# Delta-rule attention and an exact-GELU feed-forward on one core: nine runs of small matrix products fewer, K S tied tile by tile to the joins

## The chip, the cores and the metric

The kernel runs on one core of one Trainium2 chip. The metric is the device time of one execution in microseconds (us). Before the change three runs gave 630.46, 628.44 and 628.91 us, so the median is 628.91 us. Everything is computed in 32-bit floating point.

## The reference

Two layers follow each other. The first is a delta rule with a state of 48 x 48 for each of 4 x 8 heads, over 768 tokens; the second is a feed-forward layer with the exact GELU over the 3072 tokens.

```python
k_n = k / (np.linalg.norm(k, axis=-1, keepdims=True) + 1e-06)
for t in range(768):
    y[:, :, t] = q_t @ state
    state = state + beta_t * outer(kn_t, v_t - kn_t @ state)
x = y.transpose(0, 2, 1, 3).reshape(3072, 384)
h = x @ w_in                      # 384 x 2048
g = 0.5 * h * (1 + erf(h / sqrt(2)))
out = g @ w_out                   # 2048 x 384
```

## The kernel before

The 768 tokens are cut into 12 chunks of 64. For each chunk the recurrence becomes small products for each head. `grams` (L439, PSUM tile `psG`) multiplies the keys with themselves; its results go to SBUF by ACT (L601 for the later chunks). From the Gram blocks of a pair of chunks, GpSimd eliminates triangular blocks of 32; DVE then turns them (L538, L542). `join_both` puts blocks of 32 together to blocks of 64 in two levels. Both levels are products of 32 rows by 64 columns (L650, `psJ`). Level 0 is read from PSUM by eight DVE multiplications (L662, into `XM`), level 1 by eight DVE copies (L666, into `Zf`). Which of them are issued is said by `take`, one half of the heads at a time. Level 1 reads `XM`, so it follows all of L662.

With the inverse in hand a chunk `c` takes four steps. `against_state` multiplies the keys with the state and with the queries (L731, `psK`; one PSUM tile for each of the two halves of the batch); `subtract` turns it into `V` and `P` on DVE (L764, L767, L771: three instructions for each half). `solve` first multiplies the queries with the state (L751, `psQ`, copied to `y` by two ACT copies at L755), then applies the inverse (L791, `psU`, copied to `U` by ACT at L799 and L801). `outputs` computes P U and the state's update (L821 and L832, `psY`), and `turns` transposes the result (L883). These four together are `state_steps`, with further steps tied behind the solve if `second` names them.

All these products are small: they use a quarter or an eighth of TensorE's array at a time. The tiles `psG`, `psJ`, `psK`, `psQ`, `psU` and `psY` of the small products take turns in two PSUM buffers (`dn`), so that each new tile waits for the readers of the tile before the last one.

Between them stand the large products of the feed-forward layer, on the whole array. They are cut by a scheme with fewer multiplications. `part_of_layer` (L1023; tiles `psX`, `psZ`, `psY`, `psV`) does eleven products of the first layer for each block, named P1, P5, P6, P2, R22, R11, P7, P3, R12, P4, R21 in this order. After P6, DVE adds into `psY` (L1051) and then reads it again (`add_p5`, L1082); P7 accumulates into the same tile and so waits for both. After P7, DVE forms one half (L1059), and ACT applies the GELU to it; after R12 it forms another (L1071), again with a GELU behind it. `mix` (L1090, L1091 and further lines) adds and subtracts activations for the second layer (L957), whose weights and sums come ready.

The order is written out by hand: every step has a time in a list `plan` (chunk number plus a fraction), and `emit` calls the steps in the order of these times. The queues of DVE and GpSimd stand in exactly that order. TensorE's and ACT's order is the scheduler's, with two exceptions: `together` ties all TensorE instructions of its steps into one unbroken run, and `behind` keeps the large products in their own order. A loop over `w` = 4, 6, 8, 10 plans a pair of chunks each: the joins of the pair, chunk `w` and chunk `w + 1`, the Grams of chunks `w + 2` and `w + 3`. The names `begins` and `takes` hold the times of the joins, of the two chunks' steps and of the takes.

Of the kernel before, what the change touches and what calls it, by code (L numbers as in the profile page):

```python
# [19 lines left out]
def kernel(  # L20
# [35 lines left out]
    NA = B // 2  # L56
# [38 lines left out]
    tiles = {}  # L95
# [616 lines left out]

    SIDES = [(0, 0), (1, 0), (0, 1), (1, 1)]

    def against_state(us):

        for u in us:
            u.W = u.V
            u.y = None
            if u.c == 0:  # L720
                nc.gpsimd.tensor_tensor(u.W, u.V,
                                        ng[:, u.a].unsqueeze(2).to_broadcast([128, H, D]),
                                        op=ALU.mult)
                continue
            w = D if u.c == 1 else D + C
            psK = dn("psK")
            u.psK = psK[:, :, 0:NP * w].rearrange("q r (j d) -> q r j d", d=w)
            for j in range(NP):
                for r, p in QUADS:
                    rows = slice(r * C, r * C + D)  # L730
                    nc.tensor.matmul(u.psK[HALF[p], r, j, :], lhsT=u.Kt[rows, p, j, :],  # L731
                                     rhs=SQ[rows, u.a, p ^ r, j, 0:w], start=True, stop=True)
            if u.c == 1:
                u.psQ = psK[:, :, NP * D:2 * NP * D].rearrange("q r (j d) -> q r j d", d=D)
                against_queries([u])
        if us[0].c > 2:
            subtract(us)

    def against_queries(us):
# [430 lines left out]
    def at(first, last, steps):  # L1170

        total, done, timed = sum(s[0] for s in steps), 0.0, []
        for w, *step in steps:
            timed.append((first + (last - first) * (done + 0.5 * w) / total, step))
            done += w
        return timed
# [122 lines left out]
    def state_at(c, *times, first=(), second=(), last=()):  # L1299

        steps = state_steps(c, first, second, last)
        if len(times) > len(steps):
# [25 lines left out]
             at(2.7, 2.701, [(1.0, together, join1[1]), (0.0, copy_out, "join", 4)]),  # L1328
             at(2.75, 2.751, [(1.0, together, join1[2]), (0.0, copy_out, "join", 4)]),
             state_at(2, None, 2.772, 2.851, 2.906, 2.922),  # L1330
             at(2.728, 2.729, [(1.0, norms, 4), (1.0, prep, 4)]), at(3.045, 3.046, [(1.0, together, (grams, [tiles[4, a] for a in range(NA)]))])]
    plan += [at(1.07, 1.071, [(1.0, load_v, 2)]), at(2.727, 2.728, [(1.0, sum_of_w, 1, 2)]), at(2.96, 2.961, [(1.0, last_sum_of_w)]), at(3.07, 3.071, [(1.0, sum_of_w, 4)])]
    plan += [at(c + 0.958, c + 0.959, [(1.0, mix_x, c)]) for c in (2, 3, *range(4, NC, 2))]
    plan += [at(t, t + 0.1, v_steps(c)) for c in range(4, NC)
# [6 lines left out]
    for c in range(4, NC):  # L1341
        us = [tiles[c, a] for a in range(NA)]
        even = c % 2 == 0
        for name, src, t in (("Kb", k, {4: 1.8, 5: 2.73, 6: 3.25, 7: 3.55}.get(c, c - (2.9 if even else 3.6))),
                             ("Qb", q, {4: 3.2, 5: 3.9}.get(c, c - (1.4 if even else 1.29)))):
            plan += [at(t, t + 0.01, [(1.0, load_blocks, c, name, src)])]
        for name, t in (("Kn", {4: 2.1, 5: 2.74, 7: 4.24}.get(c, c - (2.1 if even else 2.84))),
                        ("Kp", {4: 3.6, 5: 4.3}.get(c, c - (0.6 if even else 0.85)))):
            plan += [at(t, t + 0.01, [(1.0, load_k, c, name)])]
        t = {4: 2.7262, 5: 2.9595, 6: 3.5, 7: 4.38}.get(c, c - (2.7 if even else 2.98))  # L1350
        plan += [at(t, t + 0.0005, [(1.0, turned_k, u) for u in us])]
        t = {4: 3.88, 5: 4.452}.get(c, c - (0.47 if even else 0.77))
        plan += [at(t, t + 0.01, [(1.0, turned_q, u) for u in us])]
    def gram(c):
        return [(grams, [tiles[c, a] for a in range(NA)])] if c < NC else []
# [4 lines left out]
    def rows_of(g, w, pieces):  # L1360
        rows = eliminate_steps(g)
        assert sum(n for n, _, _ in pieces) == len(rows)
        parts, done = [], 0
        for n, first, last in pieces:
            parts += [at(w + first, w + last, rows[done:done + n])]
            done += n
        return parts
# [6 lines left out]
    for c in (2, 3, *range(4, NC, 2)):  # L1374
# [8 lines left out]
        else:  # L1383
# [1 line left out]
            plan += [at(c + x, c + x + 0.001, [(1.0, mix, c + 1, 1, h)]) for h, x in enumerate((2.3, 2.36))]  # L1385

    plan += [at(3.19, 3.191, [(1.0, transposed, u, (1,)) for u in fourth]),
             at(3.1, 3.101, [(1.0, together, *gram(5))]),
             at(2.93, 2.931, [(1.0, norms, 5)]), at(2.961, 2.962, [(1.0, prep, 5)]),
             at(3.11, 3.111, [(1.0, finish, 4)]),  # L1390
             state_at(3, 3.367, 3.59, 3.72, 3.93)]
# [2 lines left out]
    for w in range(4, NC, 2):  # L1394
        more_to_come = w + 2 < NC
        if w == 4:
            begins = 0.21, 0.29, 0.36, 0.45, 0.53, 0.63, 0.67, 0.77, 0.86, 0.93
            takes = 0.212, 0.214, 0.292, 0.294
            n6, p6, n7, p7, f7 = 0.2, 0.26, 0.4, 0.44, 0.55
        else:  # L1400
            begins = -0.305, -0.163, -0.06, 0.08, 0.21, 0.29, 0.38, 0.52, 0.67, 0.84
            takes = -0.304, -0.303, -0.16, -0.158
            n6, p6, n7, p7, f7 = 0.15, 0.2, 0.27, 0.32, 0.44
            t = -1.555 if w > 6 else -1.44
            plan += rows_of(w // 2, w, ((1, t, t + 0.001), (1, t + 0.02, t + 0.021), (1, t + 0.03, t + 0.031),
                                        (31, t + 0.04, t + 0.84), (1, -0.42, -0.419), (1, -0.331, -0.3305),
                                        (1, -0.33, -0.3295)))
        begins = [w + t for t in begins]
        if w == 4:
            one = [tiles[w, a] for a in range(NA)]  # L1410
            plan += [[(t, (together, step)) for t, step in (
                (begins[0], (join_both, 2, 0)), (begins[1], (join_both, 2, 1)),
                (w + 0.335, *gram(w + 2)), (begins[2], (against_state, one[:1])),
                (w + 0.405, (against_state, one[1:])), (w + 0.49, *gram(w + 3)))],
                     state_at(w, None, *begins[3:6])]
        else:
            plan += [at(begins[0], begins[0] + 0.001, [(1.0, together, (join_both, w // 2, 0))]),
                     at(begins[1], begins[1] + 0.001, [(1.0, together, (join_both, w // 2, 1), *gram(w + 2))]),
                     state_at(w, *begins[2:6], second=gram(w + 3))]
        plan += [state_at(w + 1, *begins[6:], second=())]  # L1420
        plan += [at(w + t, w + t + 0.001, [(1.0, take, i % 2)]) for i, t in enumerate(takes)]
        if more_to_come:
            late_ = 0.02 if w == 4 else 0.0
            plan += spread("gram", 2, begins[1] + 0.04 + 1.5 * late_) + spread("gram", 2, begins[1] + 0.06 + 1.5 * late_)
            plan += spread("gram", 4, begins[3] + 0.04 + late_)
            plan += [at(w + n6, w + n6 + 0.001, [(1.0, norms, w + 2)]), at(w + p6, w + p6 + 0.001, [(1.0, prep, w + 2)]),
                     at(w + n7, w + n7 + 0.001, [(1.0, norms, w + 3)]), at(w + p7, w + p7 + 0.001, [(1.0, prep, w + 3)]),
                     at(w + f7, w + f7 + 0.001, [(1.0, finish, w + 2)])]
# [32 lines left out]
```

## Time and profile before

| what | value |
|---|---|
| median of three runs | 628.91 us (628.44 to 630.46) |
| the profiled execution's own time | 629.47 us |
| its span | 627.7 us |
| TensorE matmul (PE), busy | 606.6 us, 97%, 8358 records |
| VectorE (DVE), busy | 428.5 us, 68% |
| ScalarE (ACT), busy | 240.6 us, 38% |
| GpSimd (POOL), busy | 212.8 us, 34% |
| mean granted clock of TensorE | 0.986 of full speed |

The span is the stretch from the first to the last instruction that the profile shows; 1.77 us of the execution's time lie outside it. One 32-bit product is two records of a matmul, one transpose is one. [...] In the timeline a row holds consecutive instructions of one line and one tile; a mark in brackets gives the idle time before the row and what ended it.

### The profile page before, as it was taken

The page shows a single profiled execution, that of the slowest core. Times are in us where ns is not written, and L with a number is a line of the kernel's source. Part 1 is how long each engine was busy: PE and PEld are TensorE (multiplying, and loading weights), DVE is VectorE, ACT ScalarE, POOL GpSimd, SP SyncE. Part 2 cuts the span into 40 slices and gives each one's busy share as a digit, 9 for nine tenths or more (in the row PEclk, how much of TensorE's full clock was granted, in tenths as well). Part 3 has the DMA queues.
Part 4 walks back from the last instruction along what each step waited for, and adds up shares of the span by engine and source line. Part 5 has one row for each costly group of instructions (what it writes and reads, how often), then busy time and mean ns, then how long its engine had stood idle before and what let it go on. Part 6 is the DMA issues. An engine that isn't in the chain of part 4 may idle for free.

```text
span 627.7 us, 19675 instructions
## 1 busy us (share of the span) xinstructions
PE 606.6 (97%) x8358; PEld 541.4 (86%) x8358; DVE 428.5 (68%) x793; ACT 240.6 (38%) x546; POOL 212.8 (34%) x316
## 2 busy tenths in 40 slices
PE   6779999999999999999999999999999999999997
PEld 4667886776899999998899998899998899988997
DVE  6999899999867598564859555859546946422432
ACT  3476876615443255224451134452134222044200
POOL 4045002000379821885222884223884200000000
PEclk9985999999999999999999999999999999999999
DMA  9695766001423452453123533013321001000011
GB/s 135 155 284 145 162 146 180 23 3 38 74 38 47 78 92 35 69 105 39 16 45 54 101 62 38 12 33 62 64 50 18 11 2 28 8 19 1 0 26 26
DMA packets 159575, 39.63 MB, mean 63 GB/s; under 512 B 151168, under 2 KB 154368, under 8 KB 159488
## 3 DMA queue, kind: packets, MB, share of 16 engines
q1 hardware_dynamic: 156816, 37.34, 30.9%
q10 hardware_dynamic: 2672, 1.03, 0.8%
q8 instruction: 66, 1.08, 0.7%
q14 instruction: 21, 0.17, 0.1%
HBM read 33.62 MB, written 4.72 MB: 61 GB/s over the span
## 4 chain that ended last, share of the span: by engine, by line
PE 81%; DVE 10%; DMA 4%; SPq 2%; issue 1%; ACT 1%; DVEq 0%
PE psX L957 13%; PE psY L1023 11%; PE psY L957 9%; PE psX L1023 8%; PE psV L1023 6%; PE psZ L1023 5%; PE psZ L957 4%; PE psV L957 4%; PE psK L731 3%; PE psO L924 3%; PE psG L439 2%; DMA w_raw<-in_moe_w_out_dram 2%; PE psH L906 2%; PE psY L821 2%; PE psU L791 2%; PE psQ L751 2%
## 5 line engine op out<-in xcount | busy, mean ns | idle before, releaser
L376 POOL TENSOR_TENSOR n<-n,half 128x16 f32<-128x16 f32 x10 | 30.9, 3091 | 176.1 <-DVE n L374 118.4
L529 POOL TENSOR_TENSOR Nu<-Nu,tmp 128x30 f32<-128x30 f32 (+14 forms) x120 | 65.7, 548 | 9.4
L527 POOL TENSOR_TENSOR tmp<-Nu 128x30 f32<-128x30 f32 (+14 forms) x120 | 62.5, 521 | 9.4
L1023 PE MATMUL psX<-xT,w_in_sb 128*128 128x256 f32 (+1 forms) x288 | 62.5, 346 | 0.0
L957 PE MATMUL psX<-w_out_sb,G 128*128 128x192 f32 x320 | 56.4, 329 | 0.0
L957 PEld LDWEIGHTS psX<-w_out_sb,G 128*128 128x128 f32 x320 | 52.1, 190 | 0.8
L1023 PEld LDWEIGHTS psX<-xT,w_in_sb 128*128 128x128 f32 x288 | 47.9, 191 | 5.3
L906 PE MATMUL psH<-xT,w_in_sb 128*128 128x256 f32 x192 | 45.8, 395 | 0.7 <-ACT G L912 0.5
L906 PEld LDWEIGHTS psH<-xT,w_in_sb 128*128 128x128 f32 x192 | 37.1, 197 | 8.0 <-ACT G L912 1.4
L924 PE MATMUL psO<-w_out_sb,G 128*128 128x384 f32 x128 | 43.9, 490 | 0.0
L1051 DVE TENSOR_TENSOR psY<-psY,pu 128x512 f32<-128x512 f32 x20 | 14.0, 700 | 40.9 <-PE psY L1023 40.3
L1023 PE MATMUL psY<-xT,w_in_sb 128*128 128x256 f32 (+1 forms) x192 | 41.5, 345 | 0.0
L1006 ACT COPY pu<-psZ 128x512 f32<-128x512 f32 x40 | 23.5, 587 | 38.7 <-PE psZ L1023 36.3
L1006 ACT COPY xT<-psX 128x768 f32<-128x768 f32 x9 | 7.2, 799 | 81.1 <-PE psX L883 81.1
L924 PEld LDWEIGHTS psO<-w_out_sb,G 128*128 128x128 f32 x128 | 23.5, 190 | 14.2 <-issue 0.3
L1023 PEld LDWEIGHTS psY<-xT,w_in_sb 128*128 128x128 f32 x192 | 32.1, 191 | 3.5
L837 DVE TENSOR_TENSOR SQ<-SQ,psY 128x384 f32<-128x384 f32 x21 | 11.6, 552 | 32.5 <-PE psY L832 32.2
L1006 ACT ACTIVATE G<-G 128x512 f32<-128x512 f32 x40 | 25.2, 631 | 19.8 <-DVE G L1059 19.6
L1006 ACT ACTIVATE G<-psY 128x512 f32<-128x512 f32 x20 | 11.9, 596 | 47.4 <-PE psY L1023 47.4
L1059 DVE TENSOR_TENSOR G<-psY,pu 128x512 f32<-128x512 f32 x20 | 13.8, 690 | 22.2 <-PE psY L1023 21.5
L957 PE MATMUL psY<-w_out_sb,G 128*128 128x192 f32 x160 | 28.1, 329 | 0.0
L957 PE MATMUL psZ<-T,pu 128*128 128x192 f32 x160 | 28.1, 329 | 0.0
(204 smaller groups left out, 1374.6 us busy)
## 6 DMA issues: line engine op xcount, KB each, us to landing
Kp<-in_k_dram SPq DMA_DIRECT2D x76, 96.0 KB, 3.2
w_out_sb<-in_moe_w_in_dram SPq DMA_DIRECT2D x24, 256.0 KB, 5.5
w_raw<-in_moe_w_out_dram SPq DMA_DIRECT2D x16, 384.0 KB, 5.2
V<-in_v_dram SPq DMA_DIRECT2D x48, 96.0 KB, 3.1
out_dram<-o_sb SPq DMA_DIRECT2D x40, 96.0 KB, 2.2
Qp<-in_k_dram SPq DMA_DIRECT2D x64, 32.0 KB, 2.3
Qp<-in_q_dram SPq DMA_DIRECT2D x96, 16.0 KB, 2.0
Qp<-in_k_dram SPq DMA_DIRECT2D x64, 16.0 KB, 2.1
```

The costliest lines, as they stand in the source:

```text
L376: nc.gpsimd.tensor_tensor(flat, flat, half, op=ALU.pow)
L439: nc.tensor.matmul(psG[HALF[p], r, i * NP + j, :], lhsT=u.Kt[rows, p, j, :], rhs=(u.Qt if x else u.Kt)[rows, p, j, :], start=True, stop=True)
L527: rows_on.tensor_tensor(tmp, nu[:, j + 1:, j:j + 1].to_broadcast([128, n, j]), nu[:, j:j + 1, 0:j].to_broadcast([128, n, j]), op=ALU.mult)
L529: rows_on.tensor_tensor(nu[:, j + 1:, 0:j], nu[:, j + 1:, 0:j], tmp, op=ALU.add)
L731: nc.tensor.matmul(u.psK[HALF[p], r, j, :], lhsT=u.Kt[rows, p, j, :], rhs=SQ[rows, u.a, p ^ r, j, 0:w], start=True, stop=True)
L906: nc.tensor.matmul(psH, lhsT=w_in_sb[:, f // 2, m, f % 2 * 128:(f % 2 + 1) * 128], rhs=xTs[c][:, m, :], start=(m == 0), stop=(m == NM - 1))
L924: nc.tensor.matmul(u.psO, lhsT=G[:, u.a, f, :], rhs=w_out_sb[:, f, :], start=(f == 0), stop=(f == NF - 1))
L957: nc.tensor.matmul(ps_, lhsT=lhs[:, f, :], rhs=rhs[:, f, :], start=first and f == 0, stop=f == FH - 1, skip_group_check=not first)
L1006: i = fn(*args, **kw)
L1023: nc.tensor.matmul(ps_[:, i], lhsT=lhs[:, f // 2, f % 2 * 128:(f % 2 + 1) * 128], rhs=rhs, start=first and i == 0, stop=True, skip_group_c ...
L1051: nc.vector.tensor_tensor(L1["Y1"], L1["Y1"], L1["pu"][:, 0], op=ALU.add)
L1059: nc.vector.tensor_tensor(half(1, 1), shaped(L1["Y1"]), shaped(L1["pu"][:, 0]), op=ALU.add)
```

## The change

For each of the four pairs, the products K S of the even chunk are no longer a step behind both joins. Those of the first half of the batch are tied behind level 0 of the joins, those of the second half behind level 1, each in one run of TensorE. `against_state` gets an argument to leave out `subtract`, which is now planned for each half by itself: DVE's three instructions for the first half follow the eight of level 0, those for the second half follow the eight of level 1, with a few of the feed-forward's instructions between.

The Grams move as well. Those of chunk 4 are tied to those of chunk 5. In the pairs from 4 on, those of chunk `w + 2` are tied behind the solve of chunk `w` (at `w` = 6 and 8 they were behind level 1 of the joins, at `w` = 4 alone), and at `w` = 6 and 8 those of chunk `w + 3` behind the solve of chunk `w + 1` (they were behind the solve of chunk `w`). At `w` = 4 the Grams of chunk 7 stay alone. The times of the steps around them, of the ACT copies of the Grams and of one turn of the queries are set anew, and level 0 of the joins of `w` = 6, 8 and 10 stands two large products (of 128 x 256) later than before.

In the program's order of TensorE, runs of small products between large ones go from 63 to 54: one fewer at the Grams of chunks 4 and 5, five fewer in the pair 4 (two by the K S, one by the Grams, and two because the scheduler had put large products inside a join and between the two halves of `outputs` of chunk 4), and one fewer in each of the pairs 6, 8 and 10. The number of instructions is the same on TensorE, DVE, ACT and GpSimd.

```diff
-    def against_state(us):
+    def against_state(us, take_out=True):
...
-        if us[0].c > 2:
+        if us[0].c > 2 and take_out:
             subtract(us)
...
-             at(2.728, 2.729, [(1.0, norms, 4), (1.0, prep, 4)]), at(3.045, 3.046, [(1.0, together, (grams, [tiles[4, a] for a in range(NA)]))])]
+             at(2.728, 2.729, [(1.0, norms, 4), (1.0, prep, 4)])]
...
-        t = {4: 3.88, 5: 4.452}.get(c, c - (0.47 if even else 0.77))
+        t = {4: 3.88, 5: 4.425}.get(c, c - (0.47 if even else 0.83))
...
-             at(3.1, 3.101, [(1.0, together, *gram(5))]),
+             at(3.1, 3.101, [(1.0, together, *gram(4), *gram(5))]),
...
         if w == 4:
-            begins = 0.21, 0.29, 0.36, 0.45, 0.53, 0.63, 0.67, 0.77, 0.86, 0.93
-            takes = 0.212, 0.214, 0.292, 0.294
+            begins = 0.21, 0.285, 0.42, 0.56, 0.62, 0.66, 0.77, 0.86, 0.93
...
         else:
-            begins = -0.305, -0.163, -0.06, 0.08, 0.21, 0.29, 0.38, 0.52, 0.67, 0.84
-            takes = -0.304, -0.303, -0.16, -0.158
+            begins = -0.275, -0.157, 0.04, 0.17, 0.24, 0.3, 0.44, 0.58, 0.75
...
         begins = [w + t for t in begins]
+        us = [tiles[w, a] for a in range(NA)]
+        plan += [[(t + x, step) for t, level, us_ in ((begins[0], 0, us[:1]), (begins[1], 1, us[1:])) for x, step in (
+                     (0.0, (together, (join_both, w // 2, level))), (0.001, (take, 0)), (0.002, (take, 1)),
+                     (0.003, (together, (against_state, us_, False))),
+                     ((0.004 if level == 0 else 0.035 if w == 4 else 0.0865), (subtract, us_)))],
+                 [(t, step) for t, step in zip(begins[2:5], (
+                     (together, (solve, us), *gram(w + 2)), (together, (outputs, us)), (together, (turns, us))))],
+                 state_at(w + 1, *begins[5:], second=() if w == 4 else gram(w + 3))]
         if w == 4:
-            one = [tiles[w, a] for a in range(NA)]
-            plan += [[(t, (together, step)) for t, step in (
-                (begins[0], (join_both, 2, 0)), (begins[1], (join_both, 2, 1)),
-                (w + 0.335, *gram(w + 2)), (begins[2], (against_state, one[:1])),
-                (w + 0.405, (against_state, one[1:])), (w + 0.49, *gram(w + 3)))],
-                     state_at(w, None, *begins[3:6])]
-        else:
-            plan += [at(begins[0], begins[0] + 0.001, [(1.0, together, (join_both, w // 2, 0))]),
-                     at(begins[1], begins[1] + 0.001, [(1.0, together, (join_both, w // 2, 1), *gram(w + 2))]),
-                     state_at(w, *begins[2:6], second=gram(w + 3))]
-        plan += [state_at(w + 1, *begins[6:], second=())]
-        plan += [at(w + t, w + t + 0.001, [(1.0, take, i % 2)]) for i, t in enumerate(takes)]
+            plan += [[(w + 0.5095, (together, *gram(w + 3)))]]
         if more_to_come:
-            late_ = 0.02 if w == 4 else 0.0
-            plan += spread("gram", 2, begins[1] + 0.04 + 1.5 * late_) + spread("gram", 2, begins[1] + 0.06 + 1.5 * late_)
-            plan += spread("gram", 4, begins[3] + 0.04 + late_)
+            plan += spread("gram", 2, begins[2] + 0.03) + spread("gram", 2, begins[2] + 0.05)
+            plan += spread("gram", 4, w + 0.535 if w == 4 else begins[6] + 0.04)
```

More of the change, by code (lines that the diff above doesn't have):

```diff
@@ L1403 @@
             n6, p6, n7, p7, f7 = 0.15, 0.2, 0.27, 0.32, 0.44
[L1404 to L1407, printed above, removed]
+            t = -1.5 if w > 6 else -1.44
+            plan += rows_of(w // 2, w, ((1, t - 0.05 * (w > 6), t + 0.001 - 0.05 * (w > 6)), (1, t + 0.02, t + 0.021), (1, t + 0.03, t + 0.031),
+                                        (31, t + 0.04, t + 0.84), (1, -0.39, -0.389), (1, -0.29, -0.2895),
+                                        (1, -0.289, -0.2885)))
```

## The prediction

> **What bounds the kernel now.** The page comes first: its busy shares and the chain that ended last.
>
> ```profile
> PE 606.6 (97%) x8358; PEld 541.4 (86%) x8358; DVE 428.5 (68%) x793; ACT 240.6 (38%) x546; POOL 212.8 (34%) x316
> PE 81%; DVE 10%; DMA 4%; SPq 2%; issue 1%; ACT 1%; DVEq 0%
> ```
>
> TensorE is the bound, with almost no gaps after the first 160 us. So only two things count: what TensorE's row of products takes, and new waits in it. The second view is TensorE's timeline in the pair 4, where five of the nine runs go. Start to start tells the cost.
>
> ```profile
> 219.87 1.06 PE L1023 MATMUL psV<-xT,Sw 128*128 128x128 f32 x8
> 220.76 1.06 PE L1023 MATMUL psV<-xT,w_in_sb 128*128 128x128 f32 x8
> 221.75 1.16 PE L650 MATMUL psJ<-XM,G 32*64 32x64 f32 x64
> 222.84 1.16 PE L1023 MATMUL psY<-TX,w_in_sb 128*128 128x128 f32 x8
> 223.83 1.06 PE L1023 MATMUL psY<-xT,w_in_sb 128*128 128x128 f32 x8
> 224.73 1.06 PE L1023 MATMUL psX<-xT,w_in_sb 128*128 128x128 f32 x8
> ...
> 231.64 1.00 PE L731 MATMUL psK<-SQ,Kt 48*64 48x112 f32 x32 [0.16 <-DVE Zf L666]
> ...
> 245.97 0.68 PE L821 MATMUL psY<-V,P 64*64 64x48 f32 x32 [0.24 <-ACT diag L601]
> ```
>
> Eight full-array records take 0.89 (219.87 to 220.76) inside a stretch, 0.99 just before a small run and 0.99 just after one: a stretch pays 0.20 for its two ends. The two brackets are waits that are there already. The third view is the same timeline in the pair 6.
>
> ```profile
> 304.98 1.16 PE L650 MATMUL psJ<-Zf,XM 32*64 32x64 f32 x64
> 306.07 1.16 PE L439 MATMUL psG<-Kt 48*64 48x64 f32 x64
> 307.16 1.13 PE L1023 MATMUL psX<-xT,w_in_sb 128*128 128x256 f32 x4
> ...
> 318.75 1.15 PE L751 MATMUL psQ<-SQ 48*64 48x48 f32 x64
> 319.72 1.25 PE L791 MATMUL psU<-V,Zf 64*64 64x48 f32 x64
> 320.90 1.16 PE L439 MATMUL psG<-Kt 48*64 48x64 f32 x64
> 321.99 2.87 PE L957 MATMUL psZ<-T,pu 128*128 128x192 f32 x16
> ```
>
> psJ and psG in one run cost 1.09 each, as when alone: between products of 32 and of 64 rows a joint saves nothing. psQ to psU takes 0.97. psG behind psU adds more than its 1.09: the run lasts 3.24 where psQ and psU without it last 2.01 (342.55 to 344.56), so psG there costs 1.23. It shares its buffer with psQ and waits for the copies of psQ on ACT. The fourth view is DVE's timeline in the pair 4, then ACT's.
>
> ```profile
> 222.98 3.52 DVE L662 TENSOR_TENSOR XM<-psJ,gm 32x256 f32<-32x256 f32 x8 [0.24 <-PE psJ L650]
> 228.05 3.44 DVE L666 COPY Zf<-psJ 32x256 f32<-32x256 f32 x8
> 231.53 0.70 DVE L1051 TENSOR_TENSOR psY<-psY,pu 128x512 f32<-128x512 f32 x1
> 232.33 0.69 DVE L1082 TENSOR_TENSOR pu<-psY,pu 128x512 f32<-128x512 f32 x1
> 232.94 0.55 DVE L764 TENSOR_TENSOR V<-psK,V 128x384 f32<-128x384 f32 x1
> ```
>
> ```profile
> 238.46 0.63 ACT L1006 ACTIVATE G<-G 128x512 f32<-128x512 f32 x1 [1.26 <-DVE G L1059]
> 239.00 0.84 ACT L755 COPY y<-psQ 128x384 f32<-128x384 f32 x2
> ```
>
> From 222.98 DVE has no idle time until 235: it is full here, and ACT's copies of psQ stand behind a GELU that waits for DVE.
>
> **The runs, part by part.** Each removed run takes 0.20 of the large stretch with it. The small side saves only where like meets like.
>
> Grams of 4 and 5: now 1.09 each, apart. Tied they should behave as L821 and L832 do, whose two halves take 1.08 each apart (243.73 to 244.81, 245.97 to 247.05) and 2.02 in one run (264.54 to 266.56), a saving of about 0.15. Sum -0.35; if the second waits for something, -0.20.
>
> Pair 4, five runs: 5 x 0.20 = -1.0. Small side: the join cut by large products (0.27 + 1.07) becomes 1.09, the `outputs` halves save 0.15, one psG falls from 1.19 to 1.09: -0.5. The K S halves keep 0.93 (231.64 to 232.57). That psK behind psJ saves nothing is not shown for L650; bounds are 0 and -0.15 for each, and I take 0, since psG behind psJ saves nothing.
>
> Pairs 6 and 8: one run, -0.20; K S in two halves (2 x 0.93) instead of 1.69, +0.17. Pair 10 likewise. Three times -0.03.
>
> Together -0.35 - 1.5 - 0.1 = **-1.95**, not nine times the same saving.
>
> [...]
>
> **The waits.** Two old ones in the pair 4 go: the stretches around the brackets lose 0.23 and 0.31 against the same stretches without a wait, -0.55. New ones come from DVE, whose queue now holds, from level 0 on: eight L662, three of K S (first half), L1071, two L374, eight L666, L1051, L1082, three of K S, two L424, L1059. P7 (the third psY group) accumulates into what L1082 reads. I walk both from the start of level 0.
>
> DVE to P7: 1.23 to the first L662 (221.75 to 222.98); 3.54 to L1071; 1.53 for the three of K S (232.94 to the next row at 234.47); 0.61 for L1071; 0.92 for L374; 3.48 for L666 (228.05 to 231.53); 0.80 for L1051; 0.69 for L1082; 0.15 to a waiting TensorE (L666 ends at 231.49, psK starts at 231.64): 12.95. TensorE to P7: 1.09 + 0.93, twelve large products 2.87 (222.84 to 225.71), 1.09 + 0.93, then five groups 0.99 + 4 x 0.89: 11.47. TensorE waits **1.5**. Level 1 itself is in time: XM is complete at 1.23 + 3.52 + 0.15 = 4.90, TensorE is there at 4.89.
>
> DVE to psG, from the end of L1082 at 12.80: three of K S 1.53, less 0.08 of overlap; L424 twice 1.22; L1059 0.69; GELU 0.56 until the y copies start; these 0.84; 0.06 to psG (320.84 to 320.90). That is 17.6. TensorE: P7 12.95 + 0.99, psQ and psU 2.01, psG at 15.95. It waits **1.65** more. Behind psG stands all of TensorE, so nothing hides either wait.
>
> [...] The rows L662 and L666 come to 3.5 each for runs of 1.09. [...]
>
> At 6 and 8 P7 is clear: its large products are twice as long. But the odd Gram moves behind psU (1.23 instead of 1.09): +0.13 each. For the even one I walk again. TensorE from level 0: 1.09 + 0.93, five groups 4.53 (0.97, 3 x 0.865, 0.96, as from 299.60), 1.09 + 0.93, eight groups 7.12: psQ starts at 15.7 and is through at 16.95. DVE: L1059 waits for P7, at 12.35; then 0.61, three of K S 1.53, the mix pair L1090 and L1091 1.34 (311.71 to 313.05), so the second L1071 starts at 15.85; 0.69 and a GELU of 0.56 later, at 17.1, the y copies can start, 0.13 after psQ is through. +0.13 each. Sum **+0.5**.
>
> Moved without cost, as covers show: the ACT copies of the Grams (ACT is idle 62%), the turns L424 and L429 (the list of waits has L424 wait for a load once, 2.3; in DVE's full queue of the pair 4 that much would come on top), GpSimd's elimination (it ends at 217.5 for a level 0 at 221.75, and at 6 the transposes behind it start at 295.78, 2.7 before level 0).
>
> Sum: -1.95 - 0.55 + 1.5 + 1.65 + 0.5 = **+1.15**. On the profiled execution's 629.47 that gives 630.6; it stands 0.56 above the median, so on the median 628.91 I say **630.1**.
>
> **The rivals.** *Faster:* the two waits of the pair 4 do not appear, because DVE's chain is not as rigid as it looks. Then -1.95 - 0.55 + 0.5 = -2.0: 626.9. For it: those rows show DVE busy, but TensorE waits there now only 0.16. Against it: the order in the DVE queue is fixed by hand, and each duration has a row. Chance 0.10.
>
> *Slower:* the margin at 6 and 8 fails. In front of each L1071 stands the mix pair L1090 and L1091, which read what a GELU wrote; in the pair 4 the trace has L1090 waiting 2.40 for such a GELU (at 244.99). If the first pair waits, the GELU behind L1071, the y copies and psG are late by the same amount, and TensorE with them, since the copies are 0.13 late already. It decides from zero on; with one GELU of 0.63 at each of the two stages it is +1.3 more: 631.4. For it: no slack. Against it: at 311.71 that L1090 had no idle time before it. Chance 0.30.
>
> That the runs are not removed is excluded by the program's order, 54 for 63.
>
> **The numbers.** About 0.3%, 1.9 us, is what a measurement of this kernel can tell from no change: under 627.0 is faster, over 630.8 slower. The forecast case has 0.60, from 629.2 to 631.2 (0.15 saved at each of the eight psK behind psJ would pull it to 628.9; Grams that wait, +0.15); 0.06 of it lies beyond 630.8. So slower 0.36, faster 0.10, same 0.54. The range 627.5 to 632.0 leaves out most of the faster case and the far end of the slower one.
>
> **What would show it.** Right: psK 0.93 behind each psJ; P7 of the pair 4 with a wait of 1.5 on DVE L1082; its psG with one of about 1.7 on ACT L755; the runs of psQ, psU and psG in the later pairs at 3.2 to 3.4. Wrong: TensorE without a gap between 220 and 245 (the faster rival), or DVE idle before L1090 at the pairs 6 and 8 with psG late by half a us or more (the slower one).

## The result, and the profile after

The changed kernel takes 635.89 us (median of four runs, 635.20 to 636.80), the kernel before 628.67 (628.39 to 630.46): a ratio of 1.0106, 95% interval 1.0090 to 1.0121. It is 1.1% slower, and 3.9 above the upper end of the range that was predicted. The profiled execution took 636.43 with a span of 634.7, so 7.0 more than that of before.

The page of after, the lines on engines, the queue of TensorE's instructions and the chain that ended last:

```profile
PE 605.4 (95%) x8358; PEld 540.3 (85%) x8358; DVE 430.2 (68%) x793; ACT 240.5 (38%) x546; POOL 213.1 (34%) x316
...
q8 instruction: 66, 1.08, 0.7%
...
PE 74%; DVE 18%; issue 3%; DMA 2%; ACT 2%; SPq 1%; DVEq 0%; POOL 0%; POOLq 0%; ACTq 0%
```

The work is the same; TensorE is busy for 605.4 instead of 606.6 of a longer span. The chain has gained DVE (10% to 18%) and "issue" (1% to 3%), which is time in which an engine waited for nothing that the profile shows. The line of q8 will matter: 66 packets carried 1.08 MB of instructions, so one packet is 16 KB. TensorE's 8358 records of products, as many weight loads and 138 more (135 of them semaphore instructions) are 16,854 instructions in its trace, 255.4 for each packet. That the queue is TensorE's, and that a packet is 256 instructions, are estimates from this count.

The list of TensorE's waits from 219 to 460, in total, how often, and the longest:

```profile
PE psG L439 <- ACT y L755: 1.6, 1, 1.6
PE psG L439 <- issue: 1.5, 2, 1.4
PE psY L1023 <- DVE pu L1082: 1.1, 1, 1.1
PE psJ L650 <- DVE XM L662: 0.9, 1, 0.9
PE psX L957 <- issue: 0.5, 1, 0.5
```

Three of the five belong to the pair 4. Two were predicted (P7 for L1082, psG for the y copies), one was not (level 1 for XM). The two "issue" lines were not predicted at all. First the pair 4 on TensorE:

```profile
222.65 1.00 PE L731 MATMUL psK<-SQ,Kt 48*64 48x112 f32 x32
...
227.47 1.16 PE L650 MATMUL psJ<-Zf,XM 32*64 32x64 f32 x64 [0.94 <-DVE XM L662]
...
235.44 1.16 PE L1023 MATMUL psY<-xT,w_in_sb 128*128 128x128 f32 x8 [1.12 <-DVE pu L1082]
236.53 1.15 PE L751 MATMUL psQ<-SQ 48*64 48x48 f32 x64
237.49 1.11 PE L791 MATMUL psU<-V,Zf 64*64 64x48 f32 x64
240.16 1.16 PE L439 MATMUL psG<-Kt 48*64 48x64 f32 x64 [1.56 <-ACT y L755]
```

The runs are there as planned: psK takes 0.93 behind psJ (222.65 to 223.58). The three waits are 3.62 together where the prediction had 3.15 for two. Then the odd run of the pair 8, that of its odd chunk 9:

```profile
435.65 1.15 PE L751 MATMUL psQ<-SQ 48*64 48x48 f32 x64
436.62 1.11 PE L791 MATMUL psU<-V,Zf 64*64 64x48 f32 x64
437.79 1.02 PE L439 MATMUL psG<-Kt 48*64 48x64 f32 x50
440.18 0.52 PE L439 MATMUL psG<-Kt 48*64 48x64 f32 x14 [1.36 <-issue]
440.63 4.43 PE L957 MATMUL psV<-w_out_sb,G 128*128 128x192 f32 x16
```

In the middle of 64 equal records, after the 50th, TensorE stands still, and nobody releases it. The run takes 4.98 (435.65 to 440.63), the same run at the pair 6 takes 3.23. And psV behind it takes 4.27 (440.63 to 444.90) for the usual 2.70. The windows of that place show the clock behind it (busy time and records of each engine, then the granted clock, the DMA share and GB/s):

```profile
438.80:440.20 1.40, 0.04 (x5) 0.02 (x4) 0.96 (x5) 1.27 (x4) 0.27 (x1) 1.00 0.09 7
440.60:442.00 1.40, 1.40 (x6) 1.37 (x5) 0.00 (x0) 1.23 (x3) 1.17 (x1) 0.50 0.71 158
442.00:443.50 1.50, 1.50 (x6) 1.50 (x6) 0.00 (x0) 1.08 (x2) 0.00 (x0) 0.50 0.25 59
```

After the standstill the granted clock is 0.50; the trace's clock records give 440.43 to 443.85, a stretch of 3.41 that begins 0.25 behind the standstill's end.

To place the 7.0 I cut the span at the ten starts of psQ (chunks 2 to 11). The first row counts from the first instruction that keeps an engine busy, which is 0.31 behind the zero of the rows above. The last column is the changed kernel with 36 products more that compute nothing, at about 62 us; it is explained below.

| stage | before | after | moved by 36 tiny products |
|---|---|---|---|
| start to psQ of chunk 2 | 149.33 | 149.72 | 148.77 |
| to chunk 3 (Grams of 4 and 5 in it) | 43.40 | 42.82 | 42.78 |
| to chunk 4 (joins of the pair 4) | 44.42 | 43.68 | 43.67 |
| to chunk 5 | 22.28 | 25.14 | 26.77 |
| to chunk 6 | 59.02 | 55.29 | 55.29 |
| to chunk 7 | 23.79 | 24.70 | 23.98 |
| to chunk 8 | 69.42 | 69.51 | 69.51 |
| to chunk 9 | 23.79 | 24.49 | 23.98 |
| to chunk 10 | 68.33 | 72.82 | 69.52 |
| to chunk 11 | 22.70 | 22.70 | 22.73 |
| to the last product | 96.80 | 99.40 | 99.40 |

From the pair 6 on the starts of psQ themselves stand elsewhere in the plan, so those seven stages are compared as one sum: 363.85 before, 368.91 after, 364.41 in the last column.

### The profile page after: what moved, and what is told of

Its sections match the earlier page's. It is cut to its first block, busy times and chain, and to the rows that moved or that the text cites. A ratio compares the mean times of both kernels' runs of the same rounds, so it can differ in the third digit from the quotient of the medians.

```text
span 634.7 us, 19670 instructions
## 1 busy us (share of the span) xinstructions
PE 605.4 (95%) x8358; PEld 540.3 (85%) x8358; DVE 430.2 (68%) x793; ACT 240.5 (38%) x546; POOL 213.1 (34%) x316
## 3 DMA queue, kind: packets, MB, share of 16 engines
q10 hardware_dynamic: 2672, 1.03, 0.8%
q8 instruction: 66, 1.08, 0.7%
## 4 chain that ended last, share of the span: by engine, by line
PE 74%; DVE 18%; issue 3%; DMA 2%; ACT 2%; SPq 1%; DVEq 0%; POOL 0%; POOLq 0%; ACTq 0%
PE psX L957 13%; PE psY L1023 10%; PE psY L957 8%; PE psX L1023 7%; PE psZ L1023 5%; PE psV L1023 5%; PE psZ L957 4%; PE psV L957 4%; DVE Nu L529 3%; DVE tmp L527 3%; PE psK L731 3%; PE psO L924 3%; PE psH L906 2%; PE psY L821 2%; PE psG L439 2%
## 5 line engine op out<-in xcount | busy, mean ns | idle before, releaser
L906 PEld LDWEIGHTS psH<-xT,w_in_sb 128*128 128x128 f32 x192 | 35.6, 190 | 11.7 <-ACT G L1006 3.4
L1059 DVE TENSOR_TENSOR G<-psY,pu 128x512 f32<-128x512 f32 x20 | 13.7, 687 | 23.7 <-PE psY L1023 21.4
L957 PE MATMUL psV<-w_out_sb,G 128*128 128x192 f32 x160 | 29.5, 340 | 0.0
L957 PE MATMUL psX<-T,G 128*128 128x192 f32 x160 | 28.0, 329 | 0.0
```

Source lines behind the costliest of these rows:

```text
L906: nc.tensor.matmul(psH, lhsT=w_in_sb[:, f // 2, m, f % 2 * 128:(f % 2 + 1) * 128], rhs=xTs[c][:, m, :], start=(m == 0), stop=(m == NM - 1))
L957: nc.tensor.matmul(ps_, lhsT=lhs[:, f, :], rhs=rhs[:, f, :], start=first and f == 0, stop=f == FH - 1, skip_group_check=not first)
L1059: nc.vector.tensor_tensor(half(1, 1), shaped(L1["Y1"]), shaped(L1["pu"][:, 0]), op=ALU.add)
```

## The experiments

Two theories. **Fetch:** TensorE runs out of instructions. They come in blocks of 256 (the 66 packets for 16,854 instructions); in a run of psQ, psU and psG (192 records, 384 instructions in 3.23, so 8.4 ns for one) it eats a block in 2.2. In the packet records of the trace no packet from 150 us on starts with more than 298 instructions left ahead of the block that it brings. I count from 320 instructions, 1.25 blocks, ahead of it, which is an estimate of where the packet is called for: the three "issue" waits of the changed kernel end 3.5 to 4.2 after that point, with 1.3 to 1.9 until the packet starts, 0.9 to 1.0 for the packet, and 1.3 to 1.4 from its end until TensorE goes on. A run of small products covers 320 instructions in 2.7. So by this theory a stall appears when a block's boundary lies late in such a run, and only then. **Elimination:** the wait ahead of level 1 comes from GpSimd's start. The rival to the first is that the long runs wait for ACT or DVE, or cost this by themselves.

**The boundary is moved.** Nothing is changed but the count: tiny products ahead of the rest, or in an idle place. In the first form they stand at the very start, in front of the first transposes.

```diff
+    psW = sq("psT", NP, 128)
+    for _ in range(36):      # 16 in the second kernel, 32 in the third
+        nc.tensor.matmul(psW[0:4, 0, 0:4], lhsT=lim, rhs=lim, start=True, stop=True)
     by_hand = ExitStack()
```

The changed kernel with 36:

> The changed kernel with 36 tiny products (4 x 4) put ahead of everything on TensorE, where it waits 4.3 us for the first load. They are 144 instructions (weight loads counted), so each boundary between blocks of 256 instructions meets work that lies 144 instructions earlier. Fetch theory: the three stalls of the later pairs (0.72 at the even run of pair 6, 0.5 at the even and 1.75 at the odd run of pair 8) are TensorE out of instructions, because a block boundary lies more than 300 instructions into a run of psQ, psU and psG. Here the boundaries lie at 251 (6 even), 36 and 292 (6 odd), 177 (8 even) and 218 (8 odd), so the runs take 3.2 to 3.5 and the 3.0 go; so does the half clock behind the third stall (1.56). The profile at 632, the median at 631.5 to 632.9. Pair 4 keeps its waits of 0.94, 1.12 and 1.56. Rival: the long runs wait for ACT's copies and DVE as the slower rival of the prediction has it, or cost this by themselves; then nothing moves, 635.9.

The changed kernel with 16:

> As the run before it, with 16 tiny products, 64 instructions. Fetch theory: the boundaries lie at 331 (6 even), 372 (6 odd), 257 (8 even) and 298 (8 odd) instructions, so the stalls move: 0.5 to 1 at the even run of pair 6, 1 to 1.8 at its odd run, which had none, and none at pair 8, where the runs take 3.2 to 3.5. In all 1.5 to 2.8 and perhaps a half clock of 1.56 behind the longest: median 633 to 636. Rival (ACT's copies and DVE, or the runs by themselves): stalls stay where they were, at pair 8 above all, and 6 odd stays at 3.2; 635.9.

The kernel before with 32:

> The kernel before with 32 tiny products ahead, 128 instructions. Fetch theory: its own runs of psQ, psU and psG were spared by the place of their boundaries (232 instructions in at pair 6, 157 at pair 8). Here they lie at 360 and at 29 and 285: the run of pair 6 takes 4.2 to 5.0 instead of 3.24, that of pair 8 stays at 3.4; 1 to 1.7 more, and perhaps a half clock of 1.56: median 629.7 to 632. Rival: this kernel has no wait there, so nothing changes, 628.7.

The medians were 635.74, 637.59 and 633.89, against 629.45 of the kernel before in the same comparison. All three lie above what was expected, and they settle nothing: the tiny products waited until 5.2 to 5.5 for an instruction of ACT on the tile that they read, and up to the psQ of chunk 2 the three profiles took 156.28, 149.51 and 151.88, start-ups that differ by more than the stalls sought. From that psQ to the last product the three took 475.78, 478.67 and 475.14, where after takes 480.55 and before 473.95. The first has no "issue" wait from 219 on. The third, made from the kernel before, stalls for 1.03 in its run of the pair 6, as expected. The second has no "issue" wait at the pair 8 and one inside each run of the pair 6, the odd one of which took 3.23 in the changed kernel:

```profile
341.42 1.15 PE L751 MATMUL psQ<-SQ 48*64 48x48 f32 x64
342.39 1.11 PE L791 MATMUL psU<-V,Zf 64*64 64x48 f32 x64
343.56 1.04 PE L439 MATMUL psG<-Kt 48*64 48x64 f32 x54
345.93 0.39 PE L439 MATMUL psG<-Kt 48*64 48x64 f32 x10 [1.33 <-issue]
```

It stops after 64 + 64 + 54 records, 364 instructions; the count said 372. At the even run it stopped after 322, the count said 331. Counted in the traces, over weight loads, matmuls and TensorE's semaphore instructions, the place is exact: all nine "issue" waits of TensorE of more than 0.1 from 150 us on, in all the traces of this case, stand at instruction 192 or 193 past a multiple of 256. And at no such place does TensorE pass sooner than 1.25 after the end of the packet. That the same products stall or not by where the 256th instruction falls speaks for the fetch and against every wait for data.

**The same, with the start-up left alone.** In the changed kernel TensorE is idle for 1.52 at about 62, ahead of a product of the first layer; there the 36 products stand now. (In the kernel before it is not idle there. Up to the psQ of chunk 2 the two profiles with them took 148.77 and 148.08, without them 149.72 and 149.33, so they show no cost.)

```diff
+        if c == 0 and f == 4:
+            for psW in (sq("psW", NP, 128), sq("psW", NP, 128)):
+                for _ in range(18):
+                    nc.tensor.matmul(psW[0:4, 0, 0:4], lhsT=lim, rhs=lim, start=True, stop=True)
         for m in range(NM):
             nc.tensor.matmul(psH, lhsT=w_in_sb[:, f // 2, m, f % 2 * 128:(f % 2 + 1) * 128],
```

In the changed kernel:

> The changed kernel with the 36 tiny products put where TensorE has nothing to do at about 62 us (the trace has it idle there for 1.52, until a GELU), so that the start-up is left as it is and every boundary of 256 instructions from there on moves by 144 instructions. With the same products at the very start, the time from the first psQ to the end was 475.8, for 480.55 without and 473.95 of the kernel before, but the start-up was up to 7 longer. Fetch theory: no stall at the pairs 6 and 8 and no half clock; 3.0 to 4.6 less than the 635.9 of the changed kernel: 631.3 to 633. Rival: the stage times were a matter of that start-up; then 635.9.

In the kernel before:

> The kernel before with the same 36 tiny products at the same place. Its boundaries then lie 344 instructions into the run of psQ, psU and psG of pair 6 (232 before) and 13 and 269 into that of pair 8. Fetch theory: the run of pair 6 takes 4.1 to 4.5 instead of 3.24, that of pair 8 3.4; the median 1 higher, 629.7 to 630.5. Rival: the tiny products do nothing but shift, 628.7 to 629.4.

The changed kernel fell to 632.23 (ratio to before 1.0036, 1.0024 to 1.0048; before 629.50 here), in the range of the fetch theory. The run that took 4.98 takes 3.23 again, with all 64 records of psG in one row:

```profile
437.20 1.16 PE L439 MATMUL psG<-Kt 48*64 48x64 f32 x64
438.29 2.87 PE L961 MATMUL psV<-w_out_sb,G 128*128 128x192 f32 x16
```

The kernel before rose to 630.64 (1.0019, 1.0005 to 1.0034), 1.1 more, a little above what was expected. From the first psQ to the last product its profile takes 475.00 for 473.95, by a stall that was not there before:

```profile
319.53 0.81 PE L439 MATMUL psG<-Kt 48*64 48x64 f32 x40
321.29 0.58 PE L439 MATMUL psG<-Kt 48*64 48x64 f32 x24 [0.94 <-issue]
321.80 2.87 PE L961 MATMUL psZ<-T,pu 128*128 128x192 f32 x16
```

So the same 36 products, which compute nothing, make the one kernel 3.7 faster and the other 1.1 slower. The half clock does not go with the fetch alone: this profile of the changed kernel has none at the pair 8, but one in the pair 4, behind the waits there:

```profile
237.00:240.40 3.40, 1.84 (x109) 1.65 (x101) 3.33 (x7) 2.62 (x8) 0.00 (x0) 1.00 0.31 45
240.50:243.80 3.30, 3.30 (x18) 3.30 (x18) 0.91 (x3) 2.76 (x6) 2.46 (x1) 0.54 0.25 31
```

It lasted from 240.76 to 244.17, again 3.41, and cost the stage 1.63 (26.77 for 25.14). The other way round, the stall of 1.33 above had no half clock behind it. So a stall does not always bring one, and that the one at the pair 8 came from its stall is likely, but not shown.

**The run is cut.** In the changed kernel, without tiny products, the odd Grams of the pairs 6 and 8 stand alone, and their copies on ACT follow them.

```diff
-                 state_at(w + 1, *begins[5:], second=() if w == 4 else gram(w + 3))]
+                 state_at(w + 1, *begins[5:], second=())]
         if w == 4:
             plan += [[(w + 0.5095, (together, *gram(w + 3)))]]
+        elif more_to_come:
+            plan += [[(begins[6] + 0.08, (together, *gram(w + 3)))]]
...
-            plan += spread("gram", 4, w + 0.535 if w == 4 else begins[6] + 0.04)
+            plan += spread("gram", 4, w + 0.535 if w == 4 else begins[6] + 0.09)
```

(In the pairs 8 and 10 `t`, from which the elimination is planned, moves from -1.5 to -1.46.)

> The changed kernel without tiny products, where the Grams of chunk w + 3 at the pairs 6 and 8 are no longer tied behind the solve of chunk w + 1 but stand alone, 16 records of psV later. The runs of psQ and psU there have 256 instructions, weight loads counted, instead of 384. Fetch theory: the boundary that lay 362 instructions into the odd run of pair 8 now lies after 16 records of large products, 2.6 to 2.9, so the block is there in time: the stall of 1.75 goes, and the half clock of 1.56 behind it; one run more at each pair, 0.20 less 0.13. The stalls of the even runs (0.7 and 0.5), whose runs are as before, stay. Median 1.6 to 3 below the changed kernel's 635.9: 632.9 to 634.3. Rival: the odd Gram itself waits at that place, for a buffer or for ACT; then it waits there too and the time stays at 635.9 or goes up by 0.15.

The odd run of the pair 8 and all that follows to the psQ of chunk 10 fell from 72.82 to 69.58: stall and half clock are gone, though each Gram now pays for a run.

```profile
437.89 1.11 PE L791 MATMUL psU<-V,Zf 64*64 64x48 f32 x64
438.94 2.87 PE L957 MATMUL psV<-w_out_sb,G 128*128 128x192 f32 x16
441.73 1.16 PE L439 MATMUL psG<-Kt 48*64 48x64 f32 x64
```

The median, 634.82 (1.0092, 1.0071 to 1.0114), is 0.5 above what was expected: in this execution the even run of the pair 8, which was left as it was, waited 0.88 at the same place as in the changed kernel, behind the 29th record of psG, instead of 0.18, and the stage of the Grams of 4 and 5 had a wait of 0.72 for ACT. Here the place of a stall is fixed by the count, its size is not.

**The elimination.** The Grams of chunk 4 back in a run of their own, with the 36 products at the start.

```diff
-             at(2.728, 2.729, [(1.0, norms, 4), (1.0, prep, 4)])]
+             at(2.728, 2.729, [(1.0, norms, 4), (1.0, prep, 4)]), at(3.045, 3.046, [(1.0, together, (grams, [tiles[4, a] for a in range(NA)]))])]
...
-             at(3.1, 3.101, [(1.0, together, *gram(4), *gram(5))]),
+             at(3.1, 3.101, [(1.0, together, *gram(5))]),
```

> The changed kernel with the 36 tiny products and with the Grams of chunk 4 back where they were, in a run of their own. Theory of the elimination: the wait of 0.94 ahead of level 1 in the pair 4 comes from GpSimd, whose elimination starts 1.52 later (178.52 for 177.00) because ACT copies both chunks' Grams in a row and the copy of pu, DVE L1059 and the turn L507 stand behind them. Here the elimination starts at about 177.0, L538 no longer waits for it, the wait of 0.94 goes and one run (0.35) comes back: 0.6 faster than the kernel with the 36 products alone, 631.0 to 632.3. P7 keeps 1.1 to 1.5, psG 1.56. Rival: level 1 waits because K S of the first half now stands between the levels and DVE turns two tiles ahead of L662; then the 0.94 stays, and the time is 0.35 above that of the 36 products alone.

The median was 636.20, above what was expected, as with the other kernels that begin with tiny products; its profile reaches the psQ of chunk 2 at 154.45, against 156.28 of the kernel with the 36 products alone and 149.72 without them. The wait ahead of level 1 is gone (TensorE's timeline of this kernel):

```profile
230.77 1.06 PE L1023 MATMUL psX<-xT,w_in_sb 128*128 128x128 f32 x8
231.76 1.16 PE L650 MATMUL psJ<-Zf,XM 32*64 32x64 f32 x64
```

By stages against the kernel with the 36 products alone: 0.63 lost where the Grams are (43.40 for 42.77), 0.89 won at the joins (42.60 for 43.49), 0.25 less from the first psQ to the end, not 0.6. (The wait of level 1 was 0.76 in that profile, and P7 waited 1.12 in both.) The wait was GpSimd's, and the Grams in one run are worth more than 0.35.

**The pair 4 is mended.** Everything now stands on the kernel with the 36 products in the idle place (632.23).

> As the changed kernel with the 36 products at 62 us, and in the pair 4 the Grams of chunk 6 no longer tied behind the solve but to those of chunk 7, 1.8 later. By the walk of the prediction psG waits there for the y copies on ACT behind DVE L1059 and a GELU; without it nothing stands behind the solve, so the wait of 1.56 goes, and two Grams in one run take 2.02 for 1.23 and 1.09: 1.6 to 1.9 less than with the 36 products alone. Rival: another wait takes its place, psV or the next psY behind the solve; then about 0.3 less.

```diff
-                     (together, (solve, us), *gram(w + 2)), (together, (outputs, us)), ...
+                     (together, (solve, us), *(gram(w + 2) if w > 4 else [])), (together, (outputs, us)), ...
...
-            plan += [[(w + 0.5095, (together, *gram(w + 3)))]]
+            plan += [[(w + 0.49, (together, *gram(w + 2), *gram(w + 3)))]]
```

(The ACT copies of these Grams move to 0.493 and 0.495.) It took 630.86 (1.0019, 1.0010 to 1.0028), 1.4 less, and less was won than expected. No psG waits; instead the transposes of chunk 4 (L883) wait 0.62 for DVE L847, another wait in its place, as the rival has it. The stage to the psQ of chunk 5 takes 24.20, which is 0.94 under the 25.14 that it took without a half clock: 1.56 less 0.62. The next kernel adds two edits:

> As the run before it, with two more edits. ACT copies pu ahead of the Grams of chunk 5, so that DVE L1059 and the turn L507, and with them GpSimd's elimination, come 0.7 to 0.8 earlier; the wait ahead of level 1 in the pair 4 falls from 0.94 to 0.2. DVE's two L374 of chunk 6 (0.92) move behind P7: its wait falls by that. Together the waits before P7, 2.06 in the changed kernel, fall to 0.3 to 0.6: 1.5 to 1.7 less than without these two, 628.2 to 629.5 in all, level with the kernel before or a little faster. Rival: DVE is full for the whole stretch, so what is moved comes back as a wait of psG or of L1071; then 0.8 less or nothing.

```diff
-        put = put_off if us[0].c > 5 else lambda name, dst, src: nc.scalar.copy(dst, src)
+        put = put_off if us[0].c > 4 else lambda name, dst, src: nc.scalar.copy(dst, src)
...
-             at(3.11, 3.111, [(1.0, finish, 4)]),
+             at(3.11, 3.111, [(1.0, finish, 4)]), at(3.1135, 3.1136, [(1.0, copy_out, "gram", 4)]),
...
-            n6, p6, n7, p7, f7 = 0.2, 0.26, 0.4, 0.44, 0.55
+            n6, p6, n7, p7, f7 = 0.2, 0.42, 0.4, 0.44, 0.55
```

At this place L374 sums the squares of chunk 7 for both chunks, since they share a tile: this kernel leaves out the sums of chunk 6 and so does not compute the reference's result. Its instructions are the same in number and size, so only its time is used; the kernel after it has the right sums. It took 630.13 (1.0013, 1.0002 to 1.0023). Both waits did what was expected of them:

```profile
227.87 1.16 PE L650 MATMUL psJ<-Zf,XM 32*64 32x64 f32 x64 [0.15 <-DVE XM L662]
...
234.91 1.16 PE L1027 MATMUL psY<-xT,w_in_sb 128*128 128x128 f32 x8 [0.20 <-DVE pu L1086]
...
252.43 0.55 PE L883 MATMUL psX<-ident,V 128*128 128x128 f32 x3 [0.62 <-DVE V L847]
```

The stage to the psQ of chunk 4 fell by 1.7 (43.67 to 41.97), as expected, and the time from the first psQ to the end by 1.59 (475.03 to 473.44), the median only by 0.7. The profiles of these kernels, which are equal up to the psQ of chunk 2, reach it between 148.77 and 151.71, so the start-up can hide as much; that it did is not shown. The wait of L883 was next:

> As the kernel with the three edits of the pair 4, with DVE's L374 of chunk 6 between L1091 and L374's old neighbours so that it stands ahead of the squares of chunk 7, and with the four instructions from L323 (0.93) behind L847: the last trace had L883 waiting 0.62 for L847, behind those four. That wait goes: 0.6 less than 630.13, 629.2 to 629.8, level with the kernel before within 0.1%. Rival: TensorE is not the bound there, and psK or the next psX waits instead; then 630.

```diff
-            n6, p6, n7, p7, f7 = 0.2, 0.42, 0.4, 0.44, 0.55
+            n6, p6, n7, p7, f7 = 0.2, 0.395, 0.4, 0.44, 0.62
...
-            t = -1.5 if w > 6 else -1.44
+            t = -1.5 if w > 6 else -1.375
```

629.20 against 629.75 of before in the same comparison: ratio 0.9996, 0.9984 to 1.0009. From the first psQ to the end its profile has 472.83, before 473.95. With its waits of the pair 4 down to 0.2 each and no stall, the change is level with the kernel before.

**The parts of the change that no wait paid for, put into the kernel before.**

```diff
-             ..., at(3.045, 3.046, [(1.0, together, (grams, [tiles[4, a] for a in range(NA)]))])]
+             ...]
...
-             at(3.1, 3.101, [(1.0, together, *gram(5))]),
+             at(3.1, 3.101, [(1.0, together, *gram(4), *gram(5))]),
...
-            begins = 0.21, 0.29, 0.36, 0.45, 0.53, 0.63, 0.67, 0.77, 0.86, 0.93
-            takes = 0.212, 0.214, 0.292, 0.294
+            begins = 0.21, 0.30, 0.36, 0.45, 0.56, 0.63, 0.67, 0.77, 0.86, 0.93
+            takes = 0.212, 0.214, 0.302, 0.304
```

(With the copies of chunk 5's Grams put off as above, with f7 of the pair 4 and t of the pair 6 as in the last kernel.)

> The kernel before, K S and the Grams of the pairs 4 to 10 where they were, with the parts of the change that no wait paid for: the Grams of 4 and 5 in one run (with pu copied ahead of the second ones' copies), level 1 of the joins of the pair 4 one group of large products later, so that none stands inside it, and outputs of chunk 4 later, so that none stands between its halves. Three runs fewer. By the stage from the psQ of chunk 2 to that of chunk 3 the first was worth 0.58; the split join took 0.25 more than a whole one and a run of 0.20, the split outputs 0.15, 0.20 and a wait of 0.24. Together 1.2 to 1.6 less than the kernel before, 627.9 to 628.3. Rival: level 1 and the outputs then stand late, and the turns or K S of chunk 5 wait for them; then 0.5 less or nothing.

628.89, ratio 0.9993 (0.9980 to 1.0006): not told from no change. The rival was right: K S stands where it stood and waits for what is now later, 0.68 for DVE L666 instead of 0.16. The Grams in one run won nothing here either: their stage takes 43.26 for 43.40, with a new wait of 0.22 for ACT.

```profile
231.09 1.00 PE L731 MATMUL psK<-SQ,Kt 48*64 48x112 f32 x32 [0.68 <-DVE Zf L666]
```

## Why the prediction was wrong, step by step

By the stages, before to after, with the stalls taken from the difference to the kernel with the 36 products at 62 us:

| term | predicted | measured |
|---|---|---|
| Grams of 4 and 5 | -0.35 | -0.58 |
| pair 4: five runs and two old waits | -2.05 | -1.50 (what is left of +2.12 without 3.62) |
| pair 4: new waits | +3.15 | +3.62 (0.94, 1.12, 1.56) |
| pairs 6 to 10, runs and Grams | +0.40 | +0.56 |
| stalls of the fetch | 0 | +2.98 (0.72, 0.51, 1.75) |
| half clock behind the longest | 0 | +1.56 |
| start-up | 0 | +0.39 |
| sum | +1.15 | +7.03 |

**The step that failed** is the term for psG behind the solve: "psG there costs 1.23", and with it the +0.13 for each odd Gram. The row was right (the odd run of the pair 6 takes 3.23 in the changed kernel), but it was taken as the price of the run wherever it stands. Beside the two that were there, the changed kernel has such runs at the odd chunks of the pairs 6 and 8 (and one in the pair 4, which waits for ACT), and every boundary of 256 instructions lies elsewhere in the four of the pairs 6 and 8. The kernel before had its boundaries 232 and 157 instructions into its two runs, and no stall; moved by 144 it had one too. That was in the profile of before: a queue for instructions with its 66 packets, and in the trace a few boundaries that were passed 1.45 to 1.69 after a packet's end, where those that stall in these traces are passed after 1.3 to 1.5. None of the steps looked at it, and no rival named it; the prediction's own mark of being right, runs of 3.2 to 3.4, failed at the 4.98. The stalls are 2.98, which the prediction had at nothing. With the half clock, whose tie to the stall is not shown, it is 4.5 of the 5.9 between the 7.0 by which the span grew and the 1.15.

The trace has the blocks, 66 of 16 KB for 16,854 instructions, and it shows that TensorE can use them up before the next one is there: at 8.4 ns for an instruction a run of small products passes 320 of them, the estimate from above, in 2.7, and at the three stalls TensorE went on 3.5 to 4.2 after that point.

**The second step that failed** is a cover: "GpSimd's elimination (it ends at 217.5 for a level 0 at 221.75)", and with it "Level 1 itself is in time". The margin was read at the end of the elimination, but the change moved its start. ACT's timeline of the changed kernel:

```profile
171.52 1.25 ACT L450 COPY diag<-G 32x512 f32<-32x512 f32 x2
172.77 0.59 ACT L450 COPY G<-psG 128x512 f32<-128x512 f32 x1
...
173.88 1.25 ACT L450 COPY diag<-G 32x512 f32<-32x512 f32 x2
175.15 0.59 ACT L1006 COPY pu<-psZ 128x512 f32<-128x512 f32 x1
```

The copies of the first Grams begin 2.2 later than before (170.41 for 168.19), those of both now stand in a row, and pu behind them (175.15; before 173.63). DVE waits for pu, then turns the Grams:

```profile
175.77 0.69 DVE L1059 TENSOR_TENSOR G<-psY,pu 128x512 f32<-128x512 f32 x1 [2.35 <-ACT pu L1006]
176.38 1.99 DVE L507 STREAM_TRANSPOSE Nu<-diag 128x1024 f32<-128x1024 f32 x1
...
219.26 2.13 DVE L538 STREAM_TRANSPOSE XM<-Nu 128x1024 f32<-128x1024 f32 x1 [1.38 <-POOL Nu L533]
221.28 0.65 DVE L1059 TENSOR_TENSOR G<-psY,pu 128x512 f32<-128x512 f32 x1
221.85 1.98 DVE L542 STREAM_TRANSPOSE Zf<-Nu 128x1024 f32<-128x1024 f32 x1
223.86 3.46 DVE L662 TENSOR_TENSOR XM<-psJ,gm 32x256 f32<-32x256 f32 x8
```

GpSimd follows (before, this row began at 177.00):

```profile
178.52 2.36 POOL L512 TENSOR_TENSOR Nu<-Nu,XM 128x1024 f32<-128x1024 f32 x1 [3.66 <-DVE Nu L507]
```

So L538 is late, and the first L662 begins 2.30 behind level 0 (221.56 to 223.86) instead of the 1.23 of the walk. The prediction took the 4.3 between the end of the elimination and level 0 as free, but L538 (2.02), L1059 (0.57) and L542 (2.01, each from start to start) follow each other there. In the profile of before they ran from 217.98 to 222.73, and the first L662 began at 222.98: the cover was these 0.25 and the 0.5 by which L538 stood behind the elimination, not 4.3; the change took 1.5. With the copies in the other order the wait ahead of level 1 was 0.15.

**What held.** psK behind psJ cost 0.93. Wait by wait the walks of DVE's and ACT's queue were close: P7 waited 1.12 and level 1 0.94 ahead of it, 2.06 for 1.5, where the 0.94 is the other step's (with the Grams of chunk 4 put back, P7 waited 1.12 alone); psG 1.56 for 1.65. Moving L374 behind P7 took 0.92 from P7's wait, its own length, so DVE's chain was as rigid as said and the faster rival had no ground. That rival and the slower one both fell: psG at the even runs of the pairs 6 and 8 came 0.12 late for the copies of psQ, 0.13 in the walk, and L1090 did not wait there. The change of the pairs 6 to 10 cost 0.56 for 0.40. Without the fetch, the half clock and the 0.94 the table comes to +1.55, and to +1.16 without the start-up, which no edit touches; that this is the predicted +1.15 is in part luck, since the runs of the pair 4 saved less than thought and the Grams more.

## What to carry to other kernels

A long run of small products is bounded by instructions as well as by data: count them (weight loads and semaphore instructions too), find where each 256th falls, and keep the boundaries out of the last part of the run (here those counted 321 to 395 instructions behind its start stalled, the last of them just behind its end, and those counted at 13 to 298 did not), or put a large product ahead of it (with psV there the stage of 72.82 took 69.58, stall and half clock gone); moving the count by instructions in an idle place settles whether a stall of "issue" is this. A cover is good only for the whole chain behind it: if a change moves the start of an elimination, walk its end and every instruction that stands between it and the place that needs it. And a run that is removed saves its joint only if the products behind it do not then wait: three runs fewer in the kernel before won nothing that could be measured, since K S waited 0.68 instead.

## What the runs showed of the hardware

Small products of a quarter of the array, at 8.4 ns for an instruction, outrun the fetch of their own instructions: stalls of 0.18 to 1.36 without any releaser, within ten instructions of the counted boundary (at the same place of the 256, to one instruction, with the semaphore instructions counted), and of differing size at one place (0.18 and 0.88 for the same record). A place that stalls can be moved by tiny products alone, in both directions: the same 36 took a stall of 1.36 out of one kernel and put one of 0.94 into the other.

Twice, between 150 and 600 us in all the traces, a stretch of 3.41 at a granted clock of 0.50 stood behind a standstill among small products, of 1.36 in the changed kernel and of 1.55 at the pair 4 with the 36 products at 62 us; it cost 1.56 and 1.63. The stall of 1.33 had none behind it, and the same three waits of the pair 4 had it behind them in one profile of five, so the standstill alone does not decide it. In the 3.41 ahead of the two stretches TensorE was idle for 1.42 and 1.56; what sets such a stretch off is not shown. The four times of the changed kernel (635.20, 635.35, 636.43, 636.80) would fit one such stretch more or less, but only the profiled one, 636.43, is known to have had it.
